# An attention and mixture-of-experts kernel on one core: register loads, weight fetches, a laid-out order of steps and the last tile, changed together

## The chip, the cores and the metric

The kernel runs on one core of a Trainium2 chip. The metric is the device time of one execution in microseconds. It is given as the median of several runs of the same program. A profile is one further execution, recorded by the hardware profiler; its times are counted from the first instruction of the program (the span's start).

The engines are named as in the profile: PE multiplies matrices and PEld loads its weights, DVE, ACT and POOL work on vectors, SP issues transfers. A name with q behind it (SPq, ACTq) is the sequencer of that engine, which waits, branches, reads registers and issues transfers. "Bank" is one of the eight 2 KB slices per partition of the memory into which PE writes.

## The reference

One sequence of 2048 rows of width 448 goes through an attention layer (16 heads of 28) and a mixture of 8 experts, of which each row takes two; a gate per row mixes the two results.

```python
x = A_x
g = _sigmoid((x * gate_w).sum(-1, keepdims=True))
a = softmax(q k^T / sqrt(28)) v @ wo          # q, k, v = x @ wqkv
logits = x @ w_gate                           # top 2 of 8, softmax over the two
b = sum over e of w[e] * (_silu(x @ w1[e]) @ w2[e])   # w1 448 x 1792, w2 1792 x 448
return g * a + (1 - g) * b
```

## The kernel before, in words

Most products are made of values split in a high and a low part of type fp32r, so one product is three matrix multiplications (high by high, high by low, low by high). The work comes in four stages, one behind the other on PE.

**First projection** (lines 366 to 393). For each of 16 tiles of 128 rows PE forms v and the logits (11 multiplications of 458 columns). The tile's x comes by `load_x` over SP into a ring of 8, ACT and DVE split it two tiles ahead (`split_xt`), ACT copies the finished v into `v_s` (a ring of 3), and SP stores that to `v_d`. The weights of the second projection come beside it in 8 pieces: `load_wq(t)` at tile t = 0 to 7 into a ring of 4, split by ACT and DVE at t = 4 to 11. Before the first tile PE turns an identity matrix `BUSY` = 20 times (line 350). POOL writes a block of zeros to `zero_d` (line 317); from it SP fills those rows of `ys_d` that no expert may write (32 transfers, line 965; they stand in the code far behind, but the scheduler orders SP itself and puts them wherever their source is there).

**Second projection** (`qk_tile`, lines 590 to 622 and 636 to 641). q and k, seven tiles of 128 columns, each in four pieces of 512 rows: 11 multiplications into one of four banks (`pq`), ACT copies the high part `hi` (ring of 3), DVE the low part `lo`, and SP stores both to DRAM (lines 614, 615). Between them DVE works out the routing: it orders the experts by how many rows they have, so that place 0 is the expert with the most. Behind the fourth tile `load_experts` (lines 219 to 222, called in line 633) reads the expert's number of every place into registers of SP, eight reads in a row, since the addresses of w1 and w2 depend on it; `load_w1` (line 224) and `fetch_w2` (line 716) use them.

**Experts** (lines 864 to 988). Eight places e, each in two halves hf of 7 blocks of 128 hidden columns. A half first forms the hidden values (the first product, line 903): per block twice 11 multiplications of 288 to 256 columns (`CAPS`: 576 rows at place 0, 512 from place 6), 154 in all, each 11 into one of two banks `acc0` and `acc1` in turn (`accumulator`); ACT takes them out with silu (`hf32`, the rows above 512 into `ht`) and POOL makes low parts. Then comes the second product (line 953): 4 tiles of 128 rows of 21 multiplications, 84 in all, again in turn into the two banks. Between the two stands, at places 0 to 5, a block that is run only where the place has more than 512 rows (`last_slots` under `tc.If(cnt > 512)`, lines 939 to 941): 28 multiplications into the bank that is next in turn. In the second halves PE also turns the next place's x (line 754).

**The maxima, laid between.** The softmax needs an upper bound per row, so every score of q and k is formed once ahead, in 1024 cells of 512 columns (`max_stream`, lines 103 to 151), during the expert stage. A step (`step`, line 194) takes 6 cells into the six banks of `pm`, of which there is one set, and DVE takes their maxima (lines 132, 138). If the step is given the accumulator that is not in use, it takes a seventh cell into it. Where 16 rows of maxima are full, the next step that is given a bank turns and stores them instead (`store_max`, a flush, line 153). Where the steps stand is written by hand: `STEPS[e][hf]` has a list for the 154 places of the first product and one for the 84 of the second; a positive number means a step with the spare accumulator behind that multiplication, a negative one a step without (`behind`, line 858).

**Attention and output** (lines 1086 to 1152): scores, exponentials and values for 16 units, then for each of 16 tiles the output product (`project`, 11 multiplications of 448 columns), one DVE instruction that adds the experts' part (`finish`) and one store.

PE, DVE and ACT run in the written order, in the expert stage POOL too. SP's order is the scheduler's, but SP too works it off one after the other.

Of the kernel before, what the change touches and what calls it, by code (L numbers as in the profile page):

```python
# [8 lines left out]
F32 = mybir.dt.float32  # L9
# [3 lines left out]
AF = mybir.ActivationFunctionType  # L13
ALU = mybir.AluOpType
# [3 lines left out]

NXT = 8
A_AT = (1, 4)  # L20
BUSY = 20


STEPS = [
# [8 lines left out]
]  # L33

S, D, H, DH, E, FF = 2048, 448, 16, 28, 8, 1792
NT = S // 128
# [10 lines left out]
NF = FF // 128  # L47
# [13 lines left out]
def tile_gated_mha_moe(ctx: ExitStack, tc: tile.TileContext, x, xT, wv, wqk, wo, w1, w2, out):  # L61
    nc = tc.nc
    out = out[0]
# [19 lines left out]
    cnt_i = consts.tile([128, 2, E], I32, name="cnt_i")  # L83
# [129 lines left out]

    w1f = w1.rearrange("e d f -> (e d) f")
    w2f = w2.rearrange("e f d -> (e f) d")
    experts = []


    def load_experts():
        for p in range(E):  # L220
            experts.append(nc.values_load(cnt_i[0:1, 1, p:p + 1], engines=[mybir.EngineType.SP],
                                          min_val=0, max_val=E - 1))

    def load_w1(p, c):
        t = pe.tile([128, 4, 256], F32, name="w1r", bufs=3)
        cs = slice(c * 256, (c + 1) * 256)
        nc.sync.dma_start(t[:, 0:3], w1f[ds(experts[p] * D, 384), cs].rearrange("(b p) n -> p b n", p=128))
        for r in (0, 64):
            nc.sync.dma_start(t[r:r + 64, 3], w1f[ds(experts[p] * D + 384, 64), cs])
        return t  # L230


# [18 lines left out]
    with ExitStack() as pa:  # L251
        sb = pa.enter_context(tc.tile_pool(name="pa_sb", bufs=1))
        wk = pa.enter_context(tc.tile_pool(name="pa_wk", bufs=3))
        ps = pa.enter_context(tc.tile_pool(name="pa_ps", bufs=4, space=PSUM))
# [59 lines left out]
        nc.gpsimd.dma_start(neg_d.rearrange("o (a n) -> o a n", a=4), bc(neg.unsqueeze(1), [1, 4, 512]))  # L314
        zf = sb.tile([128, D], F32, name="zf")
        nc.gpsimd.memset(zf, 0.0)
        nc.gpsimd.dma_start(zero_d, zf)
        sbase = sb.tile([128, E + 1], F32, name="sbase")
        nc.gpsimd.memset(sbase[:, 0:1], 0.0)
        mb = sb.tile([128, NT + 1, E], BF, name="mb")  # L320
# [4 lines left out]
        wqk_h = sb.tile([128, 4, 2 * D], F32R, name="wqk_h")  # L325
        wqk_l = sb.tile([128, 4, 2 * D], F32R, name="wqk_l")
# [39 lines left out]
        for t in range(NT):  # L366
            ts = slice(t * 128, (t + 1) * 128)
            if t != 1:
                for t_ in ((0, 1) if t == 0 else (t,)):
                    pvs[t_] = ps.tile([128, 512], F32, name="pq")[:, 0:NV]  # L370

                for t_, j in (((0, 0), (0, 1), (1, 0), (1, 1), (0, 2), (1, 2), (0, 3), (1, 3)) if t == 0 else
                              [(t, j) for j in range(4)]):
                    v_block(t_, j)
            pv = pvs.pop(t)
            if 0 < t and t + 2 < NT:
                split_xt(t + 2)
            if 4 <= t < 12:
                b, c = divmod(t - 4, 2)
                cs = slice(c * D, (c + 1) * D)  # L380
                nc.scalar.activation(wqk_h[:, b, cs], wqr[t - 4], AF.Copy)
                nc.vector.tensor_tensor(wqk_l[:, b, cs], wqr[t - 4], wqk_h[:, b, cs].bitcast(F32),
                                        op=ALU.subtract)
            v_s = wk.tile([128, H, 32], F32, name="v_s")
            nc.gpsimd.memset(v_s[:, :, DH:DH + 1], 1.0)
            nc.gpsimd.memset(v_s[:, :, DH + 1:32], 0.0)
            nc.scalar.activation(v_s[:, :, 0:DH], pv[:, 0:D].rearrange("p (h d) -> p h d", h=H), AF.Copy)
            nc.vector.tensor_copy(lg[:, t], pv[:, D:D + E + 1])
            if t + NXT - 1 < NT:
                load_x(t + NXT - 1)  # L390
            if t < 8:
                load_wq(t)
            nc.sync.dma_start(v_d[ts], v_s.rearrange("p h d -> p (h d)"))

        def tmp(name, shape, dt=F32):
            return sb.tile(shape, dt, name=name)
# [233 lines left out]
                x_tile(xgs[k], k, lambda: ps.tile([128, 4, 128], F32, name="pt"), *xe)  # L630

        next(ms)
        load_experts()
        xgs = [gather(0, k) for k in range(5)]
        w1rs = [load_w1(0, c) for c in range(3)]
        for i, mt in enumerate((5, 2, 6)):
# [68 lines left out]
    with ExitStack() as pb:  # L705
        sb1 = pb.enter_context(tc.tile_pool(name="pb_sb1", bufs=2, reuse_waits="tile"))
        sb = pb.enter_context(tc.tile_pool(name="pb_sb", bufs=2, reuse_waits="tile"))
        ps = pb.enter_context(tc.tile_pool(name="pb_ps", bufs=1, space=PSUM, reuse_waits="tile"))
# [7 lines left out]
        def fetch_w2(i):  # L716
            if i < E * NF:
                t = sb.tile([128, D], F32, name="w2r", bufs=9)
                nc.sync.dma_start(t, w2f[ds(experts[i // NF] * FF + i % NF * 128, 128)])
                w2rs.append(t)  # L720

        def split_w1_high(p, half):
# [16 lines left out]
        turn = [0]  # L739
# [84 lines left out]
        def last_slots(e, hf, hs, y):  # L824
            n, w = CTS[e][4], D // 2
            py = accumulator()
            for f in range(NH):
                w2r = w2t[e * NF + hf * NH + f][2]
                for c in range(2):
                    nc.tensor.matmul(py[64 * c:64 * c + n, 0:w], hs[f][2][:, 0:n], w2r[:, c * w:(c + 1) * w],  # L830
                                     start=f == 0, stop=f == NH - 1)
            r0 = e * CPAD + 512
            yo = sb.tile([128, D], F32, name="yo") if hf else y
            for c in range(2):
                rw = slice(64 * c, 64 * c + n)
                nc.scalar.activation(yo[rw, 0:w], py[rw, 0:w], AF.Copy)
                if hf:
                    nc.gpsimd.tensor_tensor(yo[rw, 0:w], yo[rw, 0:w], y[rw, 0:w], op=ALU.add)
                    nc.gpsimd.dma_start(ys_d[r0:r0 + n, c * w:(c + 1) * w], yo[rw, 0:w])
# [24 lines left out]
        for e in range(E):  # L864
# [10 lines left out]
            for hf in range(2):  # L875
                hs = []
                lag = None
                w1_steps, w2_steps = STEPS[e][hf]
                for f in range(NH):
                    ft = hf * NH + f  # L880
                    p = e * NP + ft // 2
# [49 lines left out]
                for n_k, k in enumerate((4, 0, 1, 2, 3)):  # L931
                    if k == 4:
                        if hf == 0 and len(CT) == 5:
                            ysb[4] = sb.tile([128, D], F32, name="ysb", bufs=5)
                        if (e, hf) == (E - 1, 1):
                            spilled()

                            nc.scalar.activation(sb.tile([128, 1], F32, name="warm", bufs=1), ident[:, 0:1], AF.Exp)
                        if len(CT) == 5:
                            with tc.If(cnt > 512):  # L940
                                last_slots(e, hf, hs, ysb[4])
                        for f in range(NH):
                            fetch_w2(base + f + 9)
                    n = 128
# [89 lines left out]
        split_xl(OT[:, :, ts], oh, ol, 128)  # L1034
        halves[t] = (oh, ol)

    def project(pa_, oh, ol):
        mms = []
        for j in range(3):
            mms += [(oh[:, j], wo_h[:, j]), (oh[:, j], wo_l[:, j]), (ol[:, j], wo_h[:, j])]  # L1040
        mms += [(oh[:, 3], wo_h[:, 3]), (oh[:, 3], wo_l[:, 3])]
        for i, (a, b) in enumerate(mms):
            nc.tensor.matmul(pa_, a, b, start=i == 0, stop=i == len(mms) - 1)  # L1043

    def finish(t, pa_, b1):
        nc.vector.scalar_tensor_tensor(b1, pa_, coef[:, 0, t:t + 1], b1, op0=ALU.mult, op1=ALU.add)  # L1046
        nc.sync.dma_start(out[t * 128:(t + 1) * 128], b1)


    def spread_sums(u, osb):  # L1050
# [91 lines left out]
            scores(n + 3)  # L1142

    for t in range(NT):
        pa_ = (ps.tile([128, 3, 512], F32, name=f"ps3{t % 2}")[:, 0] if t % 4 < 2 else
               ps.tile([128, 512], F32, name=("ps1", "po")[t % 2]))[:, 0:D]
        project(pa_, *halves.pop(t))
        if t + 4 < NT:
            split_o(t + 4, nc.scalar)
        finish(t, pa_, b1s.pop(t))  # L1150
        for k in {2: (0,), 3: (1, 2), 4: (3,)}.get(t, ()):
            divide(NG - 1, 3, k, *ended[4 * NG - 1])
# [43 lines left out]
```

## Time and profile before

| | us |
|---|---|
| median of 3 runs | 1420.41 |
| lowest, highest | 1418.54, 1420.75 |
| the profiled execution | 1414.95 |
| its span, first to last instruction | 1413.1 |
| PE busy in it | 1398.2 |
| first projection, first to last multiplication | 5.60 to 44 |
| second projection | 44.15 to 122.1 |
| experts | 122.14 to 887 |
| output product | 1372.7 to 1409.3 |

The profiled execution is 5.5 us under the median of the runs, and 1.9 us lie outside its span. A row of a timeline has start, duration, engine, line, operation, what is written and what is read; in square brackets stands how long the engine sat idle before it and what ended that. Multiplications overlap: the time that one takes of PE is the distance between two starts, not its duration. Groups have the count behind an x, then busy time and mean duration.

### The profile page before, as it was taken

Reading aid. Unit: us, or ns where it says so; the run is one execution under the profiler, and the core shown is the slowest. Engines: PE = TensorE matmul, PEld = TensorE weight load, DVE = VectorE, ACT = ScalarE, POOL = GpSimd, SP = SyncE. Lnnn points to the kernel's source line nnn. Section 1 sums busy time; section 2 is a strip of 40 time slices with the busy share of each in tenths; the row PEclk is TensorE's granted clock in tenths of the full one; section 3 lists DMA queues with packets and bytes.
Section 4 is the critical chain, followed back from the end, with each engine's and each line's share of the span. In section 5 each row is a group of like instructions: output and inputs, shape, how many; then the busy total and the mean of one; then the engine's idle time right before and its main releaser. Section 6 shows DMA issues by size and latency. Waiting matters only on the chain. (4 is left out here: it accounts for less than half of the span.)

```text
span 1413.1 us, 28682 instructions
## 1 busy us (share of the span) xinstructions
PE 1398.2 (99%) x11017; PEld 932.3 (66%) x11017; DVE 798.3 (56%) x909; ACT 913.5 (65%) x1531; POOL 644.5 (46%) x682
## 2 busy tenths in 40 slices
PE   9999999999999999999999999999999999999998
PEld 8878888888878878888788888333333333333347
DVE  5736877778787878888788776012221122211136
ACT  5325355355345444653455435999999999999981
POOL 2113586497487567775885646221121121221120
PEclk9999999999999999999999999999999999999999
DMA  9777552342342244313432220311421321141103
GB/s 341 280 249 253 164 165 64 111 121 76 97 128 69 89 145 124 93 62 109 145 103 77 90 74 32 94 49 43 124 75 42 100 81 48 44 133 55 33 24 119
DMA packets 106541, 152.81 MB, mean 108 GB/s; under 512 B 17910, under 2 KB 77379, under 8 KB 105888
## 3 DMA queue, kind: packets, MB, share of 16 engines
q1 hardware_dynamic: 97248, 129.86, 28.8%
q0 software_dynamic: 9008, 20.83, 5.1%
q8 instruction: 89, 1.46, 0.4%
q14 instruction: 52, 0.43, 0.1%
q10 hardware_dynamic: 144, 0.23, 0.1%
HBM read 115.99 MB, written 38.02 MB: 109 GB/s over the span
## 5 line engine op out<-in xcount | busy, mean ns | idle before, releaser
L138 DVE TENSOR_REDUCE mp<-pm 128x3 f32<-128x1536 f32 (+3 forms) x307 | 520.4, 1737 | 40.1 <-PE pm L118 40.1
L1096 ACT ACTIVATE P<-ps 128x1536 f32<-128x1536 f32 x254 | 367.5, 1447 | 0.0
L1105 PE MATMUL po<-P,V 128*32 128x512 f32 x2032 | 270.6, 604 | 0.0
L903 PE MATMUL acc<-xeh,w1h 128*128 128x256 f32 (+6 forms) x880 | 252.5, 296 | 0.0
L903 PE MATMUL acc<-xeh,w1l 128*128 128x256 f32 (+6 forms) x880 | 246.9, 290 | 0.4
L700 PEld LDWEIGHTS ps<-Q,Kh 29*128 29x128 f32 x2032 | 78.0, 183 | 212.5 <-ACT P L1095 212.1
L772 POOL TENSOR_TENSOR w2l<-w2r,w2h 128x448 fp32r<-128x448 f32 x112 | 129.1, 1153 | 157.7 <-ACT w2h L766 74.8
L903 PE MATMUL acc<-xel,w1h 128*128 128x256 f32 (+6 forms) x660 | 189.7, 287 | 0.0
L700 PE MATMUL ps<-Q,Kh 29*128 29x512 f32 x2032 | 189.4, 443 | 0.0
L903 PEld LDWEIGHTS acc<-xeh,w1h 128*128 128x128 f32 x880 | 165.7, 188 | 24.8 <-issue 23.7
L953 PE MATMUL acc<-w2h,hh 128*128 128x448 f32 x448 | 172.8, 386 | 3.5 <-ACT ht L909 3.3
L903 PEld LDWEIGHTS acc<-xeh,w1l 128*128 128x128 f32 x880 | 165.9, 189 | 5.5 <-issue 3.3
L953 PE MATMUL acc<-w2l,hh 128*128 128x448 f32 x448 | 166.2, 371 | 0.0
L953 PE MATMUL acc<-w2h,hl 128*128 128x448 f32 x448 | 165.4, 369 | 0.4 <-POOL hl L781 0.4
L907 ACT ACTIVATE hf<-acc 128x256 f32<-128x256 f32 (+6 forms) x224 | 86.1, 384 | 113.6 <-PE acc L903 97.2
L1109 DVE COPY osb<-po 128x512 f32<-128x512 f32 x16 | 11.1, 691 | 261.3 <-PE po L1105 227.7
L1052 POOL DMA_DIRECT2D sum_d<-osb x64 | 32.3, 520 | 267.5 <-DVE osb L1109 251.2
L1095 ACT ACTIVATE P<-ps 128x512 f32<-128x512 f32 x254 | 151.7, 597 | 1.2 <-PE ps L700 0.3
L735 POOL TENSOR_TENSOR w1l<-w1r,w1h 128x512 fp32r<-128x512 f32 (+1 forms) x88 | 138.1, 1569 | 29.3 <-ACT w1h L729 20.8
L781 POOL TENSOR_TENSOR hl<-hf,hh 128x512 fp32r<-128x512 f32 x112 | 143.9, 1292 | 0.0
L132 DVE TENSOR_REDUCE mp<-acc 128x1 f32<-128x512 f32 x110 | 76.1, 692 | 107.2 <-PE acc L118 100.6
L903 PEld LDWEIGHTS acc<-xel,w1h 128*128 128x128 f32 x660 | 124.6, 189 | 1.3 <-issue 1.1
(214 smaller groups left out, 1984.2 us busy)
## 6 DMA issues: line engine op xcount, KB each, us to landing
w2r<-in_w_dram SPq DMA_DIRECT2D x112, 224.0 KB
w1r<-in_w_dram SPq DMA_DIRECT2D x56, 384.0 KB
ys_d<-zero_d SPq DMA_DIRECT2D x32, 224.0 KB
qkh_d<-hi SPq DMA_DIRECT2D x28, 256.0 KB
qkl_d<-lo SPq DMA_DIRECT2D x28, 256.0 KB
w1r<-in_w_dram SPq DMA_DIRECT2D x112, 64.0 KB
ys_d<-yo SPq DMA_DIRECT2D x32, 224.0 KB
v_d<-v_s SPq DMA_DIRECT2D x16, 256.0 KB
```

Of the source, the lines that this page charges most:

```text
L132: nc.vector.tensor_reduce(mp[:, o:o + 1], banks[0], axis=AX.X, op=ALU.max)
L138: nc.vector.tensor_reduce(mp[:, (o + lo) % 256:(o + lo) % 256 + hi - lo], pm[:, lo:hi], axis=AX.X, op=ALU.max)
L700: nc.tensor.matmul(banks[j], k[rw, ks], q[rw, c], start=i == 0, stop=i == 2)
L735: nc.gpsimd.tensor_tensor(l[:, :, half], r[:, :, half], h[:, :, half].bitcast(F32), op=ALU.subtract)
L772: nc.gpsimd.tensor_tensor(w2l, w2r, w2h.bitcast(F32), op=ALU.subtract)
L781: nc.gpsimd.tensor_tensor(hl, hf32, hh[:, 0:512].bitcast(F32), op=ALU.subtract)
L903: nc.tensor.matmul(pu[:, 0:HC], a, b[:, cs], start=i == 0, stop=i == len(mms) - 1)
L907: nc.scalar.activation(hf32[:, hs_], pu[:, 0:nh], AF.Silu)
L953: nc.tensor.matmul(py[:n, 0:D], a[:, cs], b, start=i == 0, stop=i == 3 * NH - 1)
L1095: nc.scalar.activation(P[:, 0], p1, AF.Exp, scale=SCALE)
L1096: nc.scalar.activation(P[:, 1:4], p3, AF.Exp, scale=SCALE)
L1105: nc.tensor.matmul(po[32 * j:32 * j + 32], v[:, kt % 8, 32 * j:32 * j + 32], P[:, j] if n > 1 else P[j], start=kt == 0, stop=kt == NT - 1)
```

## The change

- `BUSY` is 18 instead of 20.
- `STEPS` no longer has a row for each place: all places have one pair of lists for the first half and one for the second. The second half of the last place has lists of its own. There are 151 entries instead of 154.
- The registers of SP are read one place at a time, where a place's number is first used (`expert(p)`).
- `zero_d` is written at tile t = 12 of the first projection instead of ahead of it, and so the 32 fills from it can't come earlier.
- The weights of the second projection are fetched at t = 3 to 10 and split at t = 7 to 14.
- At places 4 and 5 the turn of the accumulators is changed once more behind the conditional block, so that the second product begins in the bank that the block would have used.
- The last output tile is formed in two halves of 224 columns, in two banks, each with its DVE instruction and its store.

```diff
-BUSY = 20
...
-STEPS = [
-    (([-3, 28, 61, 94, -124, 149], [8, 28, 48, 68]), ([6, -36, 61, -91, 116, 148], [3, -24, 39, 58, 76])),
-    (([17, 50, 83, 116, 149], [8, 28, 48, 68]), ([6, -36, 61, -91, 116, 148], [3, -24, 39, 58, 76])),
-    (([17, 50, 83, 116, 148], [-3, -19, 35, 55, 75]), ([17, 50, 83, 116, 149], [-4, -16, -30, -46, 60, 78])),
-    (([-23, 50, 83, 116, 149], [15, 35, 55, 75]), ([17, 50, 83, 116, -148], [-9, -24, 39, 60, 78])),
-    (([-23, 50, 83, 116, 149], [15, 35, 55, 75]), ([17, 50, 83, 116, -148], [-9, -24, 39, 59, 77])),
-    (([-22, 50, 83, 116, 149], [15, 35, 55, 75]), ([17, 50, 83, 116, -150], [-10, -25, 39, 57, 77])),
-    (([-22, 50, 83, 116, 149], [18, 39, 60, 80]), ([27, 60, 93, 126], [3, -22, 37, 55, 75])),
-    (([17, 50, 83, 116, 149], [18, 39, 60, 81]), ([28, 61, 94, 127], [7, 27, 47, 67])),
-]
+BUSY = 18
...
+STEPS = (((17, 50, 83, 116, 149), (18, 38, 57, 76)), ((17, 50, 83, 116, 149), (3, -25, 39, 59, 76)))
+LAST_STEPS = ((-13, 39, 72, 105, 138), (9, 28, 47, 67))
...
-    experts = []
-
-
-    def load_experts():
-        for p in range(E):
-            experts.append(nc.values_load(cnt_i[0:1, 1, p:p + 1], engines=[mybir.EngineType.SP],
-                                          min_val=0, max_val=E - 1))
+    experts = {}
+
+
+    def expert(p):
+        if p not in experts:
+            experts[p] = nc.values_load(cnt_i[0:1, 1, p:p + 1], engines=[mybir.EngineType.SP],
+                                        min_val=0, max_val=E - 1)
+        return experts[p]
...
-        nc.sync.dma_start(t[:, 0:3], w1f[ds(experts[p] * D, 384), cs].rearrange("(b p) n -> p b n", p=128))
+        nc.sync.dma_start(t[:, 0:3], w1f[ds(expert(p) * D, 384), cs].rearrange("(b p) n -> p b n", p=128))
...
-        nc.gpsimd.dma_start(zero_d, zf)
...
-            if 4 <= t < 12:
-                b, c = divmod(t - 4, 2)
+            if 7 <= t < 15:
+                b, c = divmod(t - 7, 2)
                 cs = slice(c * D, (c + 1) * D)
-                nc.scalar.activation(wqk_h[:, b, cs], wqr[t - 4], AF.Copy)
-                nc.vector.tensor_tensor(wqk_l[:, b, cs], wqr[t - 4], wqk_h[:, b, cs].bitcast(F32),
+                nc.scalar.activation(wqk_h[:, b, cs], wqr[t - 7], AF.Copy)
+                nc.vector.tensor_tensor(wqk_l[:, b, cs], wqr[t - 7], wqk_h[:, b, cs].bitcast(F32),
...
-            if t < 8:
-                load_wq(t)
+            if 3 <= t < 11:
+                load_wq(t - 3)
             nc.sync.dma_start(v_d[ts], v_s.rearrange("p h d -> p (h d)"))
+            if t == 12:
+                nc.gpsimd.dma_start(zero_d, zf)
...
-        load_experts()
...
-                w1_steps, w2_steps = STEPS[e][hf]
+                w1_steps, w2_steps = LAST_STEPS if (e, hf) == (E - 1, 1) else STEPS[hf]
...
                         if len(CT) == 5:
                             with tc.If(cnt > 512):
                                 last_slots(e, hf, hs, ysb[4])
+
+                            if e > 3:
+                                turn[0] ^= 1
...
-    def project(pa_, oh, ol):
+    def project(pa_, oh, ol, cs=slice(0, D)):
...
-            nc.tensor.matmul(pa_, a, b, start=i == 0, stop=i == len(mms) - 1)
-
-    def finish(t, pa_, b1):
-        nc.vector.scalar_tensor_tensor(b1, pa_, coef[:, 0, t:t + 1], b1, op0=ALU.mult, op1=ALU.add)
-        nc.sync.dma_start(out[t * 128:(t + 1) * 128], b1)
+            nc.tensor.matmul(pa_[:, cs], a, b[:, cs], start=i == 0, stop=i == len(mms) - 1)
+
+    def finish(t, pa_, b1, cs=slice(0, D)):
+        nc.vector.scalar_tensor_tensor(b1[:, cs], pa_[:, cs], coef[:, 0, t:t + 1], b1[:, cs],
+                                       op0=ALU.mult, op1=ALU.add)
+        nc.sync.dma_start(out[t * 128:(t + 1) * 128, cs], b1[:, cs])
...
+        def bank(t):
+            return (ps.tile([128, 3, 512], F32, name=f"ps3{t % 2}")[:, 0] if t % 4 < 2 else
+                    ps.tile([128, 512], F32, name=("ps1", "po")[t % 2]))[:, 0:D]
+
+        pa_ = bank(t)
+        if t == NT - 1:
+
+            for h, p_ in enumerate((pa_, bank(t + 1))):
+                cs = slice(h * D // 2, (h + 1) * D // 2)
+                project(p_, *halves[t], cs)
+                finish(t, p_, b1s[t], cs)
+            continue
```

More of the change, by code (lines that the diff above doesn't have):

```diff
@@ L226, in load_w1 @@
         cs = slice(c * 256, (c + 1) * 256)
-        nc.sync.dma_start(t[:, 0:3], w1f[ds(experts[p] * D, 384), cs].rearrange("(b p) n -> p b n", p=128))
+        nc.sync.dma_start(t[:, 0:3], w1f[ds(expert(p) * D, 384), cs].rearrange("(b p) n -> p b n", p=128))
         for r in (0, 64):
-            nc.sync.dma_start(t[r:r + 64, 3], w1f[ds(experts[p] * D + 384, 64), cs])
+            nc.sync.dma_start(t[r:r + 64, 3], w1f[ds(expert(p) * D + 384, 64), cs])
         return t
@@ L718, in fetch_w2 @@
                 t = sb.tile([128, D], F32, name="w2r", bufs=9)
-                nc.sync.dma_start(t, w2f[ds(experts[i // NF] * FF + i % NF * 128, 128)])
+                nc.sync.dma_start(t, w2f[ds(expert(i // NF) * FF + i % NF * 128, 128)])
                 w2rs.append(t)
@@ L1144, in tile_gated_mha_moe @@
     for t in range(NT):
-        pa_ = (ps.tile([128, 3, 512], F32, name=f"ps3{t % 2}")[:, 0] if t % 4 < 2 else
-               ps.tile([128, 512], F32, name=("ps1", "po")[t % 2]))[:, 0:D]
+        def bank(t):
[8 more added lines that the diff above has]
+            continue
         project(pa_, *halves.pop(t))
```

## The prediction

> **What bounds the kernel now.** I read the engines' busy times first, then PE's timeline at the places where PE stands.
>
> ```profile
> PE 1398.2 (99%) x11017; PEld 932.3 (66%) x11017; DVE 798.3 (56%) x909; ACT 913.5 (65%) x1531; POOL 644.5 (46%) x682
> ...
> PEclk9999999999999999999999999999999999999999
> ```
>
> PE is busy for 99%, at a granted clock of nine tenths or more in every slice. So time comes only from less work on PE or from its few pauses. Four places hold what the change touches: a pause in each projection, the steps of the maxima, and the seam between an expert's two products.
>
> **The change part by part.** Durations come from the profiled execution: 1414.95 us, of which 1413.1 are the span. It lies 5.5 us under the median of the runs, 1420.41; the sum is made against it and carried over to the median as a difference.
>
> *Zeros and weight fetches moved.* Three rows of PE, one of ACT, two of SP's queue and one of the page's list of transfers:
>
> ```profile
> 19.96 0.37 PE L345 MATMUL pq<-xel,xh 128*128 128x458 f32 x1
> 20.82 0.48 PE L345 MATMUL pq<-xeh,xh 128*128 128x458 f32 x1 [0.50 <-ACT xh L172]
> ...
> 21.94 0.37 PE L345 MATMUL pq<-xeh,xh 128*128 128x458 f32 x1
> ...
> 19.71 0.54 ACT L387 ACTIVATE v_s<-pq 128x448 f32<-128x448 f32 x1 [5.13 <-DMA v_d<-v_s]
> ...
> 12.96 1.88 SPq L965 DMA_DIRECT2D ys_d<-zero_d  x3
> 14.96 0.99 SPq L393 DMA_DIRECT2D v_d<-v_s  x2
> ...
> ys_d<-zero_d SPq DMA_DIRECT2D x32, 224.0 KB
> ```
>
> PE waited for a split x. ACT's split stood behind `v_s`, and that stood 5.13 us for a ring buffer, whose store SP had issued only behind three fills. PE's starts from 19.96 to 21.94 lie 1.15 us further apart than four times their usual 0.21. The fills now wait for tile 12 and the fetches of wqk for tile 3, so the pause goes: **-1.15**. What is late next: the fills, from about 38 us on, beside the stores of v, q and k (rival D). The splits at t = 7 to 14 still end a tile ahead of their use.
>
> *Registers.* The reads on SP, the store behind them, and who waits:
>
> ```profile
> L221 SPq TENSOR_LOAD <-cnt_i x8: 262/268/1097, 88.0 to 93.3; - x8
> ...
> 100.16 0.53 SPq L614 DMA_DIRECT2D qkh_d<-hi  x1
> ...
> 103.24 0.60 ACT L610 ACTIVATE hi<-pq 128x512 fp32r<-128x512 f32 x1 [10.26 <-DMA qkh_d<-hi]
> ...
> 101.92 0.39 PE L601 MATMUL pq<-xh,wqk_l 128*128 128x512 f32 x1
> 104.62 0.50 PE L601 MATMUL pq<-xh,wqk_h 128*128 128x512 f32 x1 [2.31 <-DVE lo L613]
> ```
>
> Eight reads start between 88.0 and 93.3: with the arithmetic behind it one costs SP some 0.6 us, the first 1.4. Nine transfers of w1 follow, and only at 100.16 the next store of `hi`. ACT waits for its ring, and PE starts at 104.62 instead of 0.23 behind 101.92, a pause of 2.47. Without seven of the reads the store comes 4.3 us earlier, and PE's four banks never fill: **-2.45**. The seven reads come back in the expert stage, where SP fetches blocks ahead: nothing; without that cover 4.3 in all.
>
> *Head.*
>
> ```profile
> 1.42 4.53 PE L350 MATMUL pt<-ident 128*128 128x128 f32 x20 [1.42 <-DVE ident L279]
> 5.60 0.73 PE L345 MATMUL pq<-xeh,xh 128*128 128x458 f32 x1
> ...
> 4.45 0.64 DVE L337 TENSOR_TENSOR xel<-wv_r,xeh 128x458 fp32r<-128x458 f32 x1 [0.18 <-ACT xeh L336]
> ```
>
> Two turns of 0.21 fewer let PE begin 0.43 earlier; its operands are there at 5.1. The first multiplications are slower than later ones, so I take half: **-0.2** (0 to -0.43).
>
> *Steps.* One of six cells on PE and DVE, then the start of one of seven and DVE's last part of it:
>
> ```profile
> 278.98 0.29 PE L903 MATMUL acc<-xeh,w1l 128*128 128x282 f32 x1
> 279.20 0.73 PE L118 MATMUL pm<-khg,qg 28*128 28x512 f32 x6
> 279.86 0.39 PE L903 MATMUL acc<-xeh,w1h 128*128 128x282 f32 x1
> 280.09 0.29 PE L903 MATMUL acc<-xel,w1h 128*128 128x282 f32 x1
> ...
> 283.45 0.73 PE L118 MATMUL pm<-khg,qg 28*128 28x512 f32 x6
> ...
> 279.97 3.42 DVE L138 TENSOR_REDUCE mp<-pm 128x4 f32<-128x2048 f32 x2 [0.83 <-PE pm L118]
> ...
> 774.24 0.49 PE L118 MATMUL acc<-khg,qg 28*128 28x512 f32 x1
> ...
> 775.37 3.41 DVE L138 TENSOR_REDUCE mp<-pm 128x3 f32<-128x1536 f32 x2
> ```
>
> From 278.98 to 280.09 two multiplications take 1.11 us instead of 0.26, so a step costs PE 0.85. Three entries fewer: **-2.6**. But the next step can't write `pm` before DVE has read it: 283.45 is 0.06 behind 279.97 + 3.42. Behind a step of seven cells, DVE ends at 778.78, **4.6 us** behind the step's first multiplication. The new second halves have a step behind 149 of the first product and the next behind 3 of the second. What PE has between them:
>
> ```profile
> 773.41 0.28 PE L903 MATMUL acc<-xeh,w1l 128*128 128x256 f32 x1
> 773.53 0.37 PE L953 MATMUL acc<-w2h,hh 128*128 128x448 f32 x1
> ...
> 637.37 0.28 PE L903 MATMUL acc<-xeh,w1l 128*128 128x258 f32 x1
> 638.18 0.47 PE L953 MATMUL acc<-w2h,hh 128*128 128x448 f32 x1 [0.54 <-ACT ht L909]
> ...
> 637.96 0.17 ACT L909 ACTIVATE ht<-acc 128x4 f32<-128x4 f32 x1
> 638.10 0.42 ACT L910 ACTIVATE hh<-hf 128x254 fp32r<-128x254 f32 x1
> 638.71 1.06 ACT L729 ACTIVATE w1h<-w1r 128x1024 fp32r<-128x1024 f32 x1 [0.19 <-ACTq L940]
> ...
> L830 PE MATMUL acc<-w2r,ht x168: 352/352/403, 149.2 to 401.9; 128*64 128x224 f32 x56, 128*52 128x224 f32 x56, 128*40 128x224 f32 x56
> ...
> L830 PE MATMUL acc<-w2r,ht x28: 352/352/403, 149.2 to 151.7; 128*64 128x224 f32 x28
> ```
>
> At place 6 (rows of 773) it is the step's 0.85, five times 0.12 and three times 0.207 (rows of 1408, below): 2.1 us, so PE stands 2.5. Line 830 has 168 multiplications, 28 in each of six halves: the conditional block ran at places 0 to 2, where it fills the gap (28 of them from 149.2 to 151.7), and was skipped at 3 to 5. There the seam itself takes 0.7 longer (637.37 to 638.18 instead of 0.12), which leaves 1.8 of waiting at each. Together 3 x 1.8 + 2.5: **+7.9**. I walked both whole lists by this arithmetic (a flush must also wait for a last maximum and turn it, 0.5 more): other waits sum to 2.8 before and 4.0 now, **+1.2**. At these places the lists of before have 15 to 31 multiplications between the two steps.
>
> The first step of all, now behind 17 instead of 3, loses its wait for the projection's last `lo`: 122.39 to 123.76, **-1.1**.
>
> ```profile
> 122.39 0.29 PE L903 MATMUL acc<-xeh,wv_r 128*128 128x288 f32 x1
> 123.76 0.80 PE L118 MATMUL pm<-khg,qg 28*128 28x512 f32 x6 [1.07 <-DVE lo L613]
> ```
>
> *Turn of the banks at places 4 and 5.* The 0.7 is PE waiting for ACT to empty the bank it just filled (`ht` ends at 638.13). Now it takes the bank of the skipped block. Either that is free, and 0.7 go, of which DVE's and POOL's parts give some back: -0.45 for a first half. Or PE must wait until ACT has passed the end of the block: ACT's next instruction is released by its sequencer at line 940, behind `hh`, which ends at 638.52, so PE starts some 0.44 later than now. The block's reader is on ACT, and a skipped block must still count as read, so I take the second: **+0.9** for two first halves (-0.9 to +0.9); in second halves the step's wait covers it.
>
> *Last tile.*
>
> ```profile
> 1408.68 0.37 PE L1043 MATMUL po<-wo_h,oh 128*128 128x448 f32 x1
> 1408.89 0.37 PE L1043 MATMUL po<-wo_l,oh 128*128 128x448 f32 x1
> 1409.29 0.69 DVE L1046 SCALAR_TENSOR_TENSOR b<-po,coef,b 128x448 f32<-128x448 f32 x1 [1.59 <-PE po L1043]
> ...
> L1061 DVE TENSOR_TENSOR osb<-osb,rs 128x128 f32<-128x128 f32 x64 | 18.7, 292 | 2.2
> ```
>
> Eleven at 0.207 become 22 of 224 columns. No row has fp32r below 256 columns. Nearest is that one, 0.12 apart; scaled it gives 0.105, and 22 make 2.3. The only rows with 224 columns are line 830's, plain fp32, two side by side in 0.19 (149.2 to 151.7); at 0.19 each, 22 make 4.2. I take 0.11, by the row of the same type: +0.15 (0 to +1.9). DVE's last instruction shrinks from 0.69 to 0.41, on the line through 128 and 448 columns: -0.27. The smaller store I cost at nothing. Sum **-0.1**. [...]
>
> **Sum:** -1.15 - 2.45 - 0.2 - 2.6 + 7.9 + 1.2 - 1.1 + 0.9 - 0.1 = **+2.4**: 1417.35 for a profiled execution, 1422.8 for the median.
>
> **Rivals.** *B, the halves run at the fp32 price:* slower than before. It acts in the last tile alone, costs 1.8 more and decides once a multiplication of 224 columns takes over 0.13. For it: only plain fp32 is used below 256 columns here. Against it: 256 to 288 columns run in proportion. 1424.6. *C, the bank of the skipped block is free:* 1.8 less, 1421.0; against it the order of ACT's rows at 638. *D, the fills that move to 38 us and later crowd the stores of `hi`:* if those come late again by over 4 us at 100, the 2.45 isn't won: 1425.2. For it: 32 x 224 KB more move there. Against it: the store at 100.16 came some 7 us late, and PE stood only 2.5. *E, `pm` frees its banks piece by piece:* then a step need only wait for DVE's first reductions, each of the four waits shrinks by the last one's 1.7, and the kernel is faster: 1416.0. Against it: 283.45 stands behind the whole 3.42.
>
> **How the numbers follow.** The sum as it stands 0.42, B 0.20, C 0.15, D 0.16, E 0.07. A measurement can tell about 0.2%, 2.8 us, from no change, so the sum lies just inside. I give it 0.28 within and 0.14 slower. B and D are slower but for 0.02 each; C is within but for 0.02, which is faster; E is faster but for 0.01. Faster 0.08, same 0.46, slower 0.46. The sum's own range is 1421 to 1424.5. The whole range leaves out E and the far end of D: 1418.8 to 1426.3.
>
> **What would show it.** In the new profile: no pause of PE near 20 and 104; the second halves of places 3 to 6 with PE waiting for DVE's line of the maxima, 1.8 to 2.5 each, and some 4.6 between those two steps; 150 steps with cells; at places 4 and 5 a seam of over 1 us in first halves; the last 22 starts 0.11 apart. It is wrong if the pause at the third multiplication is missing, or if PE stands between 40 and 100.

## The result and the profile after

The changed kernel takes **1428.32 us** in the median of 7 runs (1425.74 to 1434.48), the kernel before 1420.66 beside it (7 runs, 1418.54 to 1421.16). The ratio is 1.0057 [1.0039, 1.0075]: slower, by 7.7 us where the forecast was 2.4, and 2.0 us beyond the end of the range. The profiled execution took 1428.61 us, 1426.4 of them the span.

The page of the kernel after, engines and the clock by slices:

```profile
PE 1403.3 (98%) x11026; PEld 934.1 (65%) x11026; DVE 799.5 (56%) x921; ACT 914.6 (64%) x1531; POOL 645.4 (45%) x682
...
PEclk9999999999999999999999999999999999999999
```

Nothing here looks different: PE is the bound, and the clock stands at 9 in each slice. A slice is 36 us long, so a drop of a few microseconds hides in a "9 or more". The mean clock of the execution tells more: 0.996 here, 1.000 in the profile before.

PE's timeline of the kernel after at place 6, second half, at the third multiplication of the second product:

```profile
774.32 0.37 PE L949 MATMUL acc<-w2h,hl 128*128 128x448 f32 x1
774.62 0.49 PE L110 MATMUL acc<-khg,qg 28*128 28x512 f32 x1
777.23 1.22 PE L110 MATMUL pm<-khg,qg 28*128 28x512 f32 x6 [2.13 <-DVE mp L130]
...
781.64 0.57 PE L949 MATMUL acc<-w2h,hh 128*128 128x448 f32 x1
782.01 0.57 PE L949 MATMUL acc<-w2l,hh 128*128 128x448 f32 x1
...
784.82 0.37 PE L949 MATMUL acc<-w2h,hh 128*128 128x448 f32 x1
785.02 0.36 PE L949 MATMUL acc<-w2l,hh 128*128 128x448 f32 x1
```

The pause is where the forecast put it, with its length: the step's other cells start 2.61 behind its first one (774.62, 777.23). In the step at the same place of the kernel before, where PE waits for nothing, it is 0.03:

```profile
774.24 0.49 PE L118 MATMUL acc<-khg,qg 28*128 28x512 f32 x1
774.27 0.73 PE L118 MATMUL pm<-khg,qg 28*128 28x512 f32 x6
```

What the forecast did not have comes behind: the multiplications of 448 columns start 0.37 apart (781.64, 782.01) instead of 0.20 (784.82, 785.02). The table by stretches, with TensorE's granted clock behind the engines' busy times, has the reason:

```profile
core 0: us, PE busy (x) PEld busy (x) DVE busy (x) ACT busy (x) POOL busy (x), PEclk, DMA share, GB/s
770.00:773.40 3.40, 3.40 (x29) 2.86 (x29) 2.59 (x4) 2.59 (x7) 3.40 (x4) 1.00 0.46 132
773.40:776.80 3.40, 1.71 (x9) 1.08 (x8) 3.40 (x3) 1.75 (x3) 3.40 (x4) 1.00 0.86 251
776.80:780.20 3.40, 2.97 (x12) 2.11 (x13) 2.59 (x4) 0.00 (x0) 3.17 (x2) 0.50 0.68 244
780.20:783.60 3.40, 3.40 (x12) 3.05 (x11) 1.80 (x3) 1.08 (x2) 1.47 (x2) 0.50 0.52 156
783.60:787.00 3.40, 3.40 (x22) 2.46 (x20) 0.00 (x0) 1.63 (x3) 1.28 (x2) 1.00 0.03 6
```

Behind the stretch in which PE stood, the clock is 0.50 for 6.83 us. That costs at most half of it, 3.4 us; against the same half with the pauses filled (a later run) it is 2.9, somewhat more than the pause itself. The profiled execution has one drop more, 3.41 us from 906.51 on, behind a pause in attention.

The seam at place 4, second half, first PE's rows, then ACT's:

```profile
584.02 0.28 PE L896 MATMUL acc<-xeh,w1l 128*128 128x264 f32 x1
585.26 0.47 PE L949 MATMUL acc<-w2h,hh 128*128 128x448 f32 x1 [0.95 <-ACTq L933]
...
586.06 0.50 PE L110 MATMUL acc<-khg,qg 28*128 28x512 f32 x1
587.38 0.73 PE L110 MATMUL pm<-khg,qg 28*128 28x512 f32 x6 [0.82 <-DVE mp L130]
...
584.75 0.41 ACT L903 ACTIVATE hh<-hf 128x248 fp32r<-128x248 f32 x1
585.36 1.06 ACT L722 ACTIVATE w1h<-w1r 128x1024 fp32r<-128x1024 f32 x1 [0.19 <-ACTq L933]
```

PE starts behind ACT's `hh`, when ACT's sequencer has passed line 933, the end of the skipped block: 1.24 us instead of 0.82. So rival C is wrong, and the reason given against it right. Two pauses stand 0.8 us apart here, 1.24 and 1.32.

The waits of PE from 100 to 890 us, of the kernel before and of the kernel after (us of idle time in total, times, longest):

```profile
PE acc L953 <- ACT ht L909: 3.3, 6, 0.5
PE pq L601 <- DVE lo L613: 2.3, 1, 2.3
PE pm L118 <- DVE lo L613: 1.1, 1, 1.1
```

```profile
PE pm L110 <- DVE mp L130: 5.2, 5, 2.1
PE acc L949 <- ACTq L933: 3.8, 4, 1.0
...
PE acc L896 <- POOL w1l L728: 1.0, 3, 0.7
```

The pause of the registers (2.3) and the first step's wait (1.1) are gone. The maxima's waits are there, and a wait for the low part of w1 on POOL, which the forecast had not.

The registers and the fills in the kernel after, and the row of PE's new pause near the start with ACT's row that releases it:

```profile
L213 SPq TENSOR_LOAD <-cnt_i x8: 263/272/901, 87.0 to 172.1; - x8
...
96.01 0.53 SPq L608 DMA_DIRECT2D qkh_d<-hi  x1
...
5.57 0.62 POOL L387 DMA_DIRECT2D zero_d<-zf  x1
...
13.28 1.25 SPq L961 DMA_DIRECT2D ys_d<-zero_d  x2
...
8.21 0.47 PE L337 MATMUL pq<-xeh,xh 128*128 128x458 f32 x1 [0.33 <-ACT xh L164]
...
7.53 0.63 ACT L164 ACTIVATE xh<-xt 128x512 fp32r<-128x512 f32 x1 [0.85 <-DMA xt<-in_xT_dram]
```

The reads are spread to 172 us, and the store of `hi` that came at 100.16 is issued at 96.01, as forecast. But `zero_d` is filled at 5.57 and the first fills are issued at 13.28 (before: 12.96): the order of instructions is the planner's, and writing the fill behind tile 12 didn't move it. The pause near 20.8 is gone all the same, and PE stands near 8 instead.

The last tile:

```profile
1421.46 0.28 PE L1039 MATMUL po<-wo_h,ol 128*128 128x224 f32 x1
1421.57 0.27 PE L1039 MATMUL po<-wo_h,oh 128*128 128x224 f32 x1
...
1423.22 0.45 DVE L1042 SCALAR_TENSOR_TENSOR b<-ps,coef,b 128x224 f32<-128x224 f32 x1 [0.78 <-PE ps L1039]
```

Halves start 0.11 apart, so rival B is wrong. From the last tile's first start to the end of the span it is 5.87 us instead of 6.24.

### The profile page after: what moved, and what is told of

Read it like the earlier page. It is cut to its first block, busy times and chain, and to the rows that moved or that the text cites. A ratio compares the mean times of both kernels' runs of the same rounds, so it can differ in the third digit from the quotient of the medians.

```text
span 1426.4 us, 28715 instructions
## 1 busy us (share of the span) xinstructions
PE 1403.3 (98%) x11026; PEld 934.1 (65%) x11026; DVE 799.5 (56%) x921; ACT 914.6 (64%) x1531; POOL 645.4 (45%) x682
## 5 line engine op out<-in xcount | busy, mean ns | idle before, releaser
L130 DVE TENSOR_REDUCE mp<-pm 128x3 f32<-128x1536 f32 (+3 forms) x301 | 510.7, 1739 | 30.1 <-PE pm L110 30.1
L124 DVE TENSOR_REDUCE mp<-acc 128x1 f32<-128x512 f32 x127 | 87.8, 692 | 127.8 <-PE acc L110 104.7
```

The lines of the kernel that those rows point to most:

```text
L124: nc.vector.tensor_reduce(mp[:, o:o + 1], banks[0], axis=AX.X, op=ALU.max)
L130: nc.vector.tensor_reduce(mp[:, (o + lo) % 256:(o + lo) % 256 + hi - lo], pm[:, lo:hi], axis=AX.X, op=ALU.max)
```

## The experiments

Two theories. **Clock:** the waits cost about what the forecast said, and on top of them come stretches at half clock that PE's pauses bring about. **Disturbance (the rival):** the clock falls now and then in any run of this program, and the waits and steps themselves cost more than was counted. The runs were made on two chips on which the kernel before has a median of 1416.9 to 1417.1 us; so ratios to it are compared, and differences within a chip. The times expected of the kernel before, of the old lists and of the two runs behind them (one list altered, all four wider) were formed against the result's 1420.66; here they count as ratios to that. For each run of each kernel there is a time and TensorE's mean clock.

### The kernel before, unchanged

> The kernel before, unchanged, for the granted clock of each run. Two theories of why the change came out 5.5 us above the sum. Clock: the sum (+2.4) was right, and what came on top is TensorE's clock, halved for one or more stretches of 3.41 us behind pauses that the change made (6.83 us behind the pause of 2.6 at place 6, in the profile after; 3.41 more at 906). Then no such pause is here: clock 1.000 to 0.998 in each run, all runs within 3 us, 1420.7. Disturbance: drops of the clock come now and then in any long run of this program, and the steps' waits themselves cost more than I counted. Then clocks of 0.992 to 0.998 show here as well, with a spread of up to 9 us like that of the changed kernel (1425.7 to 1434.5).

1416.01 us, ratio 0.9995 [0.9986, 1.0004], clocks 0.997 to 1.000, all runs within 2.9 us. So far as the clock theory said (1420.7, a ratio of 1.0000); but its profile also shows a halved stretch, behind the pause of the registers:

```profile
101.64 0.39 PE L601 MATMUL pq<-xh,wqk_l 128*128 128x512 f32 x1
104.68 0.80 PE L601 MATMUL pq<-xh,wqk_h 128*128 128x512 f32 x1 [2.66 <-DVE lo L613]
105.27 0.63 PE L601 MATMUL pq<-xl,wqk_h 128*128 128x512 f32 x1
105.70 0.63 PE L601 MATMUL pq<-xh,wqk_l 128*128 128x512 f32 x1
```

Starts are 0.43 apart behind the pause, not 0.23, and the clock is 0.50 from 104.16 on. The kernel before pays this in part of its runs; the profile that the forecast was made from was an execution without it.

### The changed kernel, unchanged

> The changed kernel, unchanged, beside the kernel before on the same chip, for the clock of each run. Clock theory: every run has a clock below 1.000, 0.992 to 0.998; each run's time less (1 - clock) times its span is nearly one number, about 1419.5 on this chip (the place6 runs at clock 1.000 took 1418.4, and their half at place 6 gained 0.75 beside the clock); median 1424.5. Disturbance: the time less the clock's part spreads as widely as the times do.

1425.31 us (1421.87 to 1430.54, 6 runs), ratio 1.0067 [1.0048, 1.0086], clocks 0.992 to 0.998. As an estimate, a stretch at half speed costs what it takes off the mean clock times the span (for the one at place 6 that is 3.4, and 2.9 were measured). Less (1 - clock) times the span, the six are 1418.4 to 1420.8: the spread of 8.7 us shrinks to 2.4, as the clock theory said. The same sum over the 7 runs of the result gives 1422.5 to 1423.9.

### The changed kernel with the old lists

```diff
-                w1_steps, w2_steps = LAST_STEPS if (e, hf) == (E - 1, 1) else STEPS[hf]
+                w1_steps, w2_steps = STEPS[e][hf]
```

(with the old table STEPS)

> The changed kernel with the old lists of steps, all else as changed. By my arithmetic of waits this takes back 7.9 + 1.2, and gives three steps (2.6) and the first step's wait (1.1) again: 5.4 less. Clock: the halved stretches go too, 5.2 in the median (each run's 1 - clock times its span): 1417.7, clock 1.000 to 0.998. Disturbance: 5.4 less alone, 1422.9, with clocks and spread as in the changed kernel. If the other edits (flip, registers, fills, halves) carry the loss, it stays near 1428.

1413.08 us (8 runs within 1.6 us, all clocks 1.000), ratio 0.9972 [0.9961, 0.9982]. Faster than the kernel before: the lists carry the whole loss. The clock theory had 0.9979, the disturbance 1.0016. Against the changed kernel's 1.0067 it is 0.95%, some 13.5 us, even more than both parts of the clock theory (10.6).

### One list altered at place 6

```diff
+                if (e, hf) == (6, 1):
+                    w1_steps, w2_steps = (17, 50, 83, 116, 149), (9, -26, 41, 60, 76)
```

> The changed kernel with one list altered: place 6's second half has its steps of the second product at 9, 26, 41, 60, 76 instead of 3, 25, 39, 59, 76. By the arithmetic the pause of 2.6 shrinks to 0.8, the whole half gains 1.65. Clock: the stretch of 6.83 us at half speed behind it goes as well, 3.4 more: 1423.3, no halved clock near place 6, the fastest runs near 1420.7; the spread shrinks, since the pauses of 1.3 to 1.7 at places 3 to 5 stay and may halve the clock in some runs. Disturbance: 1.65 less alone, 1426.7, with clocks as in the changed kernel.

1421.43 us, ratio 1.0034 [1.0020, 1.0048]. Four of 11 runs have clock 1.000, at 1418.2 to 1418.7; the others have 0.994 to 0.999 and go up to 1427.3. As ratios the clock theory had 1.0019 and the disturbance 1.0043, so the time alone decides nothing; the clocks say that the pause at place 6 is one source of the drops. That the pairs of pauses at places 3 to 5 are others, no profile shows: it is concluded from the next run, where they are gone and the drops too. The half itself shrank from 52.46 to 48.30 in the profiles. With the pauses filled and no drop it takes 49.55 (below), so 2.9 went by the clock and 1.25 by the wait, not 1.65.

### All four second halves laid out wider

```diff
+                if 3 <= e < 7 and hf:
+                    w1_steps, w2_steps = (17, 50, 83, 116, 148), (9, -26, 41, 60, 76)
```

> The changed kernel with the second halves of places 3 to 6 laid out wider: 148 instead of 149 in the first product, then 9, 26, 41, 60, 76 instead of 3, 25, 39, 59, 76. Same number of steps (150). By the arithmetic all four pauses behind the third multiplication go (none over 0.8 is left), 6.7 less in sum. Clock: with the 5.2 of the halved stretches 1416.4, clock 1.000 to 0.998 in each run. Disturbance: 1421.6 with clocks as in the changed kernel.

1418.06 us, ratio 1.0011 [1.0002, 1.0020], clocks 1.000 in ten runs of 11 and 0.999 in one. The clock's part is gone. But the time isn't that of the clock theory: as ratios it had 0.9970 and the disturbance 1.0007. The waits gained less than I had worked out: the expert stage takes 770.3 us here and 773.2 in the run with the pauses filled, both without a drop, so 2.9 and not 6.7. PE's waits name another resource:

```profile
PE acc L110 <- ACT xf L751: 2.2, 4, 0.6
```

A step with a seventh cell writes into the bank that the tile of x just turned still holds, until ACT has emptied it (`xf`): at 491.50 PE has waited 0.56 for that. The old lists have negative entries at those places, steps that take no bank; I had read the sign only as six cells instead of seven.

### The same, with steps that take no bank

```diff
+                if 3 <= e < 6 and hf:
+                    w1_steps, w2_steps = (17, 50, 83, 116, 148), (-9, -24, 39, 60, 78)
+                if (e, hf) == (6, 1):
+                    w1_steps, w2_steps = (17, 50, 83, 116, 148), (9, -26, 41, 60, 76)
```

> As the run named spread, but the first two steps of the second product at places 3 to 5 take no bank of the accumulators (9, 26, 41, 60, 76 become -9, -24, 39, 60, 78). By the arithmetic of maxima alone both are equal, so without a further wait this stays at 1418.1. Bank theory: in spread PE waited 2.2 in sum for ACT to empty the bank into which the next tile of x is turned (0.6 at each of four places), because the step wants the same bank; at places 3 to 5 this goes: 1.7 less, 1416.4, and the profile's waits on xf shrink from 2.2 to about 0.6.

1415.36 us, ratio 0.9989 [0.9980, 0.9998]: 2.7 less than the run named spread (3.1 by the ratios), 1.7 expected. The wait that was named shrank as it should:

```profile
PE acc L110 <- ACT xf L751: 0.6, 1, 0.6
```

The halves at places 3 to 5 fell from 50.33, 49.96 and 49.85 to 48.87, 49.17 and 48.39 in the profiles, within 0.5 of those with the old lists (48.59, 48.67, 47.98). The rest of the gain has a second cause, for the later steps moved too. In spread the step at 41 stands one multiplication ahead of the next tile, and PE can't begin that until DVE has read the seventh cell out of its bank: at 502.15 PE's weight load has waited 0.43 for DVE's `mp`, and the same start is 0.41 late at each of places 3 to 6. With the step at 39 it isn't late.

So the banks are a limit of their own that the forecast of these two lists left out. In the changed kernel itself PE doesn't wait for `xf`; no row of its waits has it. That wait came with the step's move from 3 to 9.

### PE kept at work in the pauses

```diff
+                        if hf and n_k == 1 and f == 0:
+                            for _ in range({3: 6, 4: 4, 5: 4, 6: 10}.get(e, 0)):
+                                nc.tensor.matmul(py[:n, 0:D], hh[:, cs], w2h, start=True, stop=True)
```

> The changed kernel with idle time filled: in the second halves of places 3 to 6 the first multiplication of the second product is done 6, 4, 4 and 10 times more (each overwrites the one before, so the result is the same), right ahead of the third multiplication at which PE waits for VectorE. The waits end when they did, only PE works in them. Clock theory: what the waits themselves cost stays and the halved stretches go: clock 1.000 in nearly every run, some 1419.5, 6 less than the changed kernel's 1425.3 on these chips, and all runs within 3 us. Rival (the waits and the steps cost it all, and the clock falls for other reasons): 1425 and clocks of 0.992 to 0.998 as before.

1420.16 us (9 runs within 1.3 us, clocks 0.999 to 1.000), ratio 1.0026 [1.0016, 1.0036]. On the same chip as the unchanged changed kernel: **5.15 us less for 24 multiplications more**. The waits end when they did: the halves at places 3 to 5 last 50.78, 50.24 and 50.03 (50.76, 50.25, 50.03 in the changed kernel's second profile). Place 6 in its timeline, and by stretches:

```profile
775.24 1.20 PE L950 MATMUL acc<-w2h,hh 128*128 128x448 f32 x5
...
776.98 0.50 PE L110 MATMUL acc<-khg,qg 28*128 28x512 f32 x1
777.53 0.73 PE L110 MATMUL pm<-khg,qg 28*128 28x512 f32 x6
...
779.95 0.36 PE L952 MATMUL acc<-w2h,hh 128*128 128x448 f32 x1
780.15 0.37 PE L952 MATMUL acc<-w2l,hh 128*128 128x448 f32 x1
```

```profile
773.40:776.80 3.40, 3.40 (x21) 2.98 (x18) 3.40 (x3) 1.94 (x4) 3.40 (x4) 1.00 0.79 250
776.80:780.20 3.40, 3.35 (x21) 2.37 (x20) 3.18 (x4) 0.66 (x2) 3.40 (x2) 1.00 0.78 283
```

PE repeats one multiplication until 776.27, the step's other cells start 0.55 behind the first instead of 2.61, and the multiplications behind it are 0.20 apart, at clock 1.00. The half at place 6 takes 49.55 instead of 52.59 (the changed kernel's second profile). This decides between the theories: no step, no wait and no list was changed, only the idleness.

### How long a pause halves the clock

A kernel by itself: bursts of multiplications, and between them pauses of 0.6 to 2.9 us, made by a chain of VectorE's instructions.

> No part of the computation: 70 bursts of 46 to 62 multiplications (128x128 by 128x512), and between two bursts PE waits for a chain of VectorE's instructions, in 14 lengths, five times each, so that PE stands for some 0.8 to 4.2 us; zeros are stored. It measures which pauses halve the clock. Window theory, from the two drops in the profile after (they begin 226 and 264 times 3.4133 us behind the start of the full clock, and 1.9 to 2.4 us of the window before each were idle, while 1.5 to 1.8 idle in a window didn't do it): none up to 1.7 us, a share that grows with the length between 1.8 and 3.6 us, by where the pause falls, all beyond some 3.8. Each drop lasts one or two windows of 3.41 us and costs half of them. [...]

In its one execution 16 of 69 pauses halved the clock. Every halved stretch begins a whole number of times 3.4133 us behind the start of the full clock and lasts 3.41 us. (In the profile of the kernel after the two drops begin 771.41 and 901.12 us behind it, 226 and 264 times 3.4133.) In these bursts it isn't the pause's length that decides but how much of it falls into one of those windows (idle time is counted from 0.22 us behind the last start before the pause):

```
idle in one window, us   pauses   halved
up to 1.69                   41        0
1.81 to 2.01                 10        0
2.02 to 2.06                  4        2
2.10 to 2.86                 14       14
```

Two pauses of the same length, 2.86 us, each in two windows and the clock of the next:

```profile
205.93:209.34 3.41, 0.73 (x4) 0.33 (x3) 2.29 (x7) 0.00 (x0) 1.00 0.00 0
209.34:212.75 3.41, 3.41 (x9) 2.64 (x9) 0.00 (x0) 0.00 (x0) 0.50 0.00 0
```

```profile
608.70:612.11 3.41, 1.71 (x8) 1.09 (x6) 1.53 (x5) 0.00 (x0) 1.00 0.00 0
612.11:615.52 3.41, 2.43 (x11) 2.03 (x12) 0.77 (x3) 0.00 (x0) 1.00 0.00 0
615.52:618.94 3.42, 3.42 (x17) 2.84 (x16) 0.00 (x0) 0.00 (x0) 1.00 0.00 0
```

The first lies in one window, and the next has 0.50; the second is cut in two, and no window falls. So one program can meet the drops in some runs and not in others, if the windows lie elsewhere. In the two profiles of the kernel before they do: in the first, with the full clock from 7.29 us on, a window ends at 102.86 and cuts the pause of the registers into 0.72 and 1.76, and the clock stays at 1.00; in the second one ends at 104.16, has 2.30 of the pause, and the next has 0.50. My window theory had the threshold at 1.8 to 1.9; in these bursts it is 2.02 to 2.10, six tenths of a window. In the kernel after it may lie a little lower: the window from 773.39 to 776.80 ahead of its drop has 1.97 idle by the same count. The cells of a step use 28 of 128 rows, which the bursts do not try. None of the 16 needed a whole idle window: the longest idle time in one was 2.86 us.

### Single edits on the kernel before

SP's registers alone (`expert(p)` in place of `load_experts()`):

> The kernel before with SP's registers loaded a place at a time, and nothing else changed. By the prediction the pause of 2.47 at 104 goes and nothing comes back: 1414.5. Clock theory: that pause halved the clock too in part of the runs of the kernel before (one of its two profiles shows a half stretch of 3.41 us that begins at 104.16), worth 1.7 each time: 1413.7, and the clocks of 0.997 to 0.999 that most runs of before show become 1.000.

1411.88 us, ratio 0.9967 [0.9955, 0.9980], clocks 0.999 to 1.000, all runs within 0.8 us. That is 4.7 us by the ratio, twice the 2.45 of the prediction: the pause went, and with it the halved stretch that followed it in part of the runs. In the two profiles of the kernel before, the experts begin 2.75 us later than here without such a stretch and 4.15 us later with one. The pause itself isn't the same in each execution either: PE idles 2.31 and 2.66 in these two, and 3.40 in the next run's profile.

The fills and fetches alone:

> The kernel before with the fill of zero_d behind tile 12 and the fetches of wqk three tiles later, and nothing else changed. By the prediction the pause near 20.8 goes: 1.15 less, 1415.9. By the traces since: the planner issues the fills where they were (13.3 instead of 13.0 us), the pause near 20 goes, but in three of four profiles PE stood 1.3 at 8 us instead, for the second tile of x, so 0 to 1.15 less with the median near 1416.6.

1416.88 us, ratio 1.0003 [0.9994, 1.0012]: nothing gained. In its profile the registers' pause has grown:

```profile
102.60 0.39 PE L602 MATMUL pq<-xh,wqk_l 128*128 128x512 f32 x1
106.39 0.50 PE L602 MATMUL pq<-xh,wqk_h 128*128 128x512 f32 x1 [3.40 <-DVE lo L614]
```

PE stands 3.40 there instead of 2.3. One profile can't say whether it always does; alone, the edit's time is in any case that of before.

### Old lists and no turn of the banks

> The changed kernel with the old lists and without the turn of the banks at places 4 and 5: what is left are SP's registers, the moved fetches and fills, BUSY 18 and the last tile's halves. The turn costs 0.4 to 0.5 in each of four halves by the traces (45.36, 48.67, 45.09, 47.98 us with it, 44.94, 48.28, 44.59, 47.56 without): 1.7 less than old_steps, 1411.4. If PE only waited there for what comes later anyway, the time stays at 1413.1.

**1410.92 us** (5 runs within 0.3 us, all clocks 1.000), ratio 0.9959 [0.9946, 0.9972]: faster than both kernels. Without the turn 0.13% less than with it, 1.8 us.

### The new lists at place 0 alone

> As the run named old_no_turn (1410.9), with the new lists at place 0 alone, and in the last half the steps at 20, 49, 79, 108, 138 and 9, 28, 47. By the arithmetic one step less and no waiting of the first step (1.1): 2.0 less, 1408.9. If the new lists cost as such, wherever they stand, it is not below 1410.9.

1410.38 us, ratio 0.9958 [0.9944, 0.9972]: no different from 0.9959, where 2.0 less was expected. In the profiles place 0 gains 2.6 (48.77 + 51.96 instead of 50.39 + 52.96), and the last half, which takes one step more, gives back 1.95 (47.85 instead of 45.90). The new lists aren't bad wherever they stand; a step that is dropped early has to be made late.

## Why the prediction was wrong, point by point

- **The step that failed is the price of the new waits.** "+7.9" priced PE's pauses at their length, and what they set off was put at nothing, without a reason. The length was right: at the four places named, the step's other cells start 1.7, 1.3, 1.3 and 2.6 late, 6.9 in sum, and 7.7 with the 0.4 that the longer seam takes of the wait at places 4 and 5. What they set off is 5.15 us of halved clock, which keeping PE busy took away with nothing else changed. The quoted row of the clock, nine tenths in each slice, could not have shown it.
- **"Other step waits +1.2"** was too small: 3.7. The lists cost 9.9 us in the expert stage's traces (the changed kernel's second profile against the old lists). Of that 3.0 are the drop at place 6 and 6.9 the four waits, and -2.6 -1.1 are the steps and the first wait; so 3.7 are others. The 16 steps that flush make most of it: they take 15.9 us of PE with the new lists and 13.7 with the old ones, 2.2 more; why, no run tried. In the last half some 0.6 to 0.9 is the wait for POOL's `w1l`. The rest, some 0.6 to 0.9, was not traced. So far the rival theory, that the steps cost more than was counted, was right too.
- **Three steps fewer, -2.6.** The profile of after has 150 steps with cells, as said. Four halves that lost one step and nothing else are 0.4 to 1.2 shorter than with the old lists, 0.86 in the mean: right.
- **First step, -1.1:** its wait is gone from the list of waits. Right.
- **Registers, -2.45.** Right in the place and too small: 4.7. In part it is the omission of the first point, with the other sign; in part the pause was longer in other executions than in the one profile that the sum used.
- **Fills and fetches, -1.15.** Wrong: 0.0 alone. "The fills now wait for tile 12" took the order of the text for the order of issue. The pause near 20.8 goes, and in five of ten profiles with this edit PE idles 0.3 to 1.2 us near 8 instead, for the second tile of x (its split starts at 7.53 in the row above).
- **Turn of the banks, +0.9** for two halves: 0.42 at each of four seams in the traces, so 0.8 for the two first halves; in the second halves the step's wait is shorter by as much. It is 1.8 in the times with the old lists, where no wait covers the second halves. Mechanism right, and rival C wrong.
- **Head and last tile, -0.3:** the old lists without the turn are 1.0 below the registers alone, with the fills in it. Right in sign and too small. The 224 columns take 0.11 each, as the sum had it. Scaling gave 105 ns, and the 22 starts are 111 ns apart.
- **The base.** The sum stood on a profile at clock 1.000 and was carried over to a median of which part was itself lost to halved stretches.
- **Rivals:** B, C and E are wrong by the rows above. D's mechanism isn't seen in the changed kernel (the store of `hi` comes at 96.01). None had the clock.

Together: 2.4, +5.15 for the clock, +2.5 for other waits of the lists, +1.15 for the fills, less 2.25 for the registers, 0.7 for the ends and 0.2 for the four waits: some 8.1. Measured were 7.7 in the result and 9.5 on the second chip (by the ratio 1.0067). The terms come from different runs, so it is a rough account.

What stays open: the profile of after has two more pauses in attention, 2.8 us at 904 and 1.7 at 1068; none of the other profiles has them, and their cause was not found. A drop follows the first of them too, so not each drop of the changed kernel need come from its lists. Nor was it tried why the drop at place 6 lasts two windows and those of the bare bursts one.

## What to carry to other kernels

A pause of the bounding engine was not worth its length alone here: with PE kept at work in four pauses that last as long as before, the run took 5.15 us less. So on PE, ask also how much of 3.41 us a pause leaves idle (2.1 and more halved the clock in the bursts), together with its neighbours, and look at the mean clock of every run, not at the slices. That two short pauses close together are as bad as a long one is my estimate; no profile shows it. Spare multiplications in an unavoidable pause can be cheaper than the pause, as the 24 here were. A list of steps has to be walked for each resource that a step takes, not only for the one that it is made for (the banks cost 2.2 us of waits in spread), and a line moved in the text of a planned program has moved nothing until the order of issue shows it (the first fills at 13.28 instead of 12.96).

## What the runs showed of the hardware

- In the bursts the clock halved behind each window of 3.41 us with 2.1 us or more of idle time in it, and behind none with less than 2.02; in the kernel after, behind one with 1.97. The drops lay on a grid of 3.4133 us (226 and 264 times it behind the start of the full clock in the kernel after), and in the two profiles of the kernel before the grid lies differently: a window ends at 102.86 in one and at 104.16 in the other. By its 3.41 us at clock 0.50, one halved window costs at most 1.7 us, an estimate; the two behind the pause at place 6 cost 2.9 to 3.0.
- In the changed kernel, with the four pauses of its lists, the run's time spreads over 8.7 us with the same work; the 9 runs with the pauses filled lie within 1.3.
- PE could not begin in the bank of a skipped conditional block until ACT's sequencer was behind the block: 0.42 us a seam.
